# An FFN behind a chunked recurrence on one core: selections on GpSimd that wait for VectorE, C set apart on ScalarE, and a new order of the program

## The chip, the cores and the metric

One core of a Trainium2 chip runs the whole program. The metric is the device time of one execution in microseconds; of several executions the median is taken. TensorE's granted clock was 1.00 throughout the profiled execution.

## What is computed

A state-space recurrence over 4 batches x 8 heads x 768 positions (head size 32, state size 16), in chunks of 32 positions, and then a feed-forward layer over the 3072 tokens of 256 values that it gives. All inputs and the output are fp32. Cut to what matters:

```python
log_a = np.log(np.clip(a, 1e-06, 1.0))
for c in range(nc):                                   # chunks of 32 positions
    cum = np.cumsum(la, axis=-1)
    L = np.exp(cum[:, :, :, None] - cum[:, :, None, :]) * causal
    M = np.einsum('bhin,bhjn->bhij', Cc, Bc) * L
    y_intra = np.einsum('bhij,bhjd->bhid', M, xc)
    y_inter = np.einsum('bhin,bhnd->bhid', Cc, state) * np.exp(cum)[:, :, :, None]
    y[:, :, sl] = y_intra + y_inter
    state = decay_full * state + sum_j (Bc x xc * decay_from_j)
h = x @ w_in                                          # x: y as 3072 x 256; w_in 256 x 2048
g = np.maximum(h, 0.0) + np.log1p(np.exp(-np.abs(h)))
return g @ w_out                                      # w_out 2048 x 256
```

## The kernel before

**Tiling.** The recurrence is cut into 24 units of 128 positions, six for each batch (unit i is batch i // 6, step i % 6). Units 0 to 7 go one by one, from 8 on in pairs. The feed-forward part takes the tokens in six blocks of 512 and the 2048 inner features in 16 tiles of 128. To keep fp32's precision every operand is split into a high and a low part (xh and xl, wih and wil, gh and gl, woh and wol), and each product is three matmuls (high by high, low by high, high by low). Blocks 0 and 1 are done directly; blocks 2 to 5 by a scheme with seven products in place of eight, whose words are a, k, b, c and e.

**What sets the order.** `ORDER` is a string of 1308 words, and the loop at the end of the file calls one function for each word, with the numbers in the word as arguments. Every engine runs its instructions in the order in which the words issue them; across engines only data, buffers and PSUM banks hold things back. `BANKS` gives the PSUM bank of each result. Words that occur several times (D, M, G, P, W and others) run one stage of their function each time.

**The words around the change.** Of a unit i:
- A (`apart`): a copy of C with every other head cleared, parts_c. `A_KIND` says for each unit who does it: "1" VectorE, "0" ScalarE, "2" ScalarE for two units at once.
- S (`score`): the scores of C and B on TensorE, from un (the unit's inputs; head_in for units 0 to 3) and parts_c.
- D (`decays`): the decays with all that is not causal set to zero, rm from fc, by GpSimd's selection: four parts of 128 x 256 for units 0 and 1, two of 128 x 512 for the others. rm has two buffers.
- M (`weigh`): m = scores x rm, two operations on VectorE, one input in PSUM and one in SBUF.
- B and C (`scale_b`, `scale_c`): B and C scaled by decays, bp and cc. T (`spread`): the state at two places, tb. U and N: the state's update. All on VectorE, apart from cc of a few early units.
- R and I (`read`, `within`), for pairs E and J: the output y of a unit on TensorE, from cc and tb, and from m and un.
- G and X, for pairs Y: y times its growth on VectorE (y, yy), the cast to xh on ScalarE, the rest xl = y - xh on VectorE.

Of the feed-forward part: W splits a tile of weights (w and wil or wol on VectorE, wih or woh on ScalarE); H and F are first-layer products, H for 256 of a block's 512 tokens (H2 and H3: feature tiles 2 and 3); P is softplus (e on ScalarE), its cast gh on ScalarE and the rest gl = e - gh on VectorE; Z is a second-layer product; F0.4 is block 0, feature tile 4. Words w, un, v and gg issue loads on SyncE's queue.

All engine operations are recorded at line 173, that of the helper which keeps them in order, so a row is told apart by its tiles.

Of the kernel before, what the change touches and what calls it, by code (L numbers as in the profile page):

```python
# [50 lines left out]
kc B23 ends la warm9 loga loga ft0 lr gb logr logr kb ft0 ft0 ft0 hc0 growth growth fr0 gq0 gq0 hc1 A0 S0 A1 D0  # L51
D0 D0 fr0 fr0 D0 ft0 un0 B0 gq2 hc3 M0 M0 un1 hc2 D1 D1 fr0 C1 warm1 B1 gq2 U0 U0 T1 C2 S1 D1 D1 un6 B6 I0 M1
warm1 G0 M1 U6 fr2 U6 A2 S3 R1 warm1 un4 C4 I1 A4 w2 W2 B4 warm1 warm1 D3 D3 M3 M3 un5 A5 C5 W2 W2 fr2 U1 U1 G1
G1 G0 S2 ft2 ft2 ft2 ft2 ft2 T2 R2 un2 B2 U2 C3 A6 D2 M2 D2 gd M2 I2 un3 B3 U3 U4 X1 U2 G2 T12 U3 S4 U4 warm2 T4
# [65 lines left out]
Z4.14.0 L4.0 ez256.15 es ez256.7 eo256 ez0.7 ez0.15 eo0 C12  # L120
# [886 lines left out]
```

## Time and profile before

| | before |
|---|---|
| median of 3 runs | 313.34 us (313.25 to 313.62) |
| profiled execution | 314.09 us |
| its span | 312.3 us |
| TensorE busy | 305.3 us (98%), 2279 matmuls |
| VectorE busy | 260.6 us (83%), 529 operations |
| ScalarE busy | 180.2 us (58%), 336 operations |
| GpSimd busy | 45.3 us (15%), 62 operations |

1.8 us of the profiled execution lie outside its span. The span has three parts. Up to about 23 us the inputs land, the decays are worked out and the first units of the recurrence run; TensorE's matmuls there are small. From 23 to about 133 us the rest of the recurrence runs between the products of blocks 0 and 1, on all engines. From then to 307 us there are only the feed-forward part's products, with the sums and the splitting that they need. A busy share of an engine is an average over these three, and GpSimd works in the first two alone.

A row of the timeline gives start, duration, engine, operation and tiles; in brackets how long the engine had been idle before it, and what ended that. A longer duration of an operation of the same shape means that it stood still while it ran.

### The profile page before, as it was taken

To read this page: it belongs to the slowest core of one execution; us is meant where nothing else is said; L and a number is where in the kernel's file an instruction comes from. 1 tells how busy PE (TensorE), PEld (TensorE's weight loads), DVE (VectorE), ACT (ScalarE), POOL (GpSimd) and SP (SyncE) were. 2 spreads that over 40 slices of the span, in tenths; PEclk is the share of its full clock that TensorE was granted. 3 is DMA by queue.
4 is the path that set the end of the run, shared out by engine and by line. 5 is a ranking of instruction groups with operands and counts; after the bars stand their busy time and mean duration, and the time that the engine had idled before them with its cause. 6 is when DMAs were issued, how large, how long until landed. Compare 5 with 4: busy or idle time off the path is not lost.

```text
span 312.3 us, 5865 instructions
## 1 busy us (share of the span) xinstructions
PE 305.3 (98%) x2279; PEld 244.4 (78%) x2279; DVE 260.6 (83%) x529; ACT 180.2 (58%) x336; POOL 45.3 (15%) x62
## 2 busy tenths in 40 slices
PE   8989999999999999999999999999999999999995
PEld 4757876887787878788888888888888888888884
DVE  5899999568699799978899968999868888777773
ACT  4947875497235734265754565556655556654561
POOL 1952722302422055000000000000000000000000
PEclk9999999999999999999999999999999999999999
DMA  6989856340653110200010000000001100000003
GB/s 185 315 234 319 277 190 198 111 144 3 188 152 98 56 44 36 70 1 0 0 69 0 0 2 0 1 0 2 0 35 67 36 0 0 1 2 0 0 0 136
DMA packets 14172, 23.21 MB, mean 74 GB/s; under 512 B 1344, under 2 KB 10176, under 8 KB 14144
## 3 DMA queue, kind: packets, MB, share of 16 engines
q1 hardware_dynamic: 14144, 22.84, 22.7%
q8 instruction: 18, 0.29, 0.4%
q14 instruction: 10, 0.08, 0.1%
HBM read 19.29 MB, written 3.54 MB: 73 GB/s over the span
## 4 chain that ended last, share of the span: by engine, by line
PE 62%; DVE 2%; issue 0%
PE sums_at L173 62%; DVE gl L173 0%; DVE xl L173 0%; DVE bp L173 0%; DVE yy L173 0%; DVE parts_c L173 0%; DVE wol L173 0%; DVE end_sum L173 0%
## 5 line engine op out<-in xcount | busy, mean ns | idle before, releaser
L173 DVE TENSOR_TENSOR gl<-e,gh 128x512 fp32r<-128x512 f32 x96 | 65.2, 693 | 19.0 <-ACT gh L173 18.8
L173 PE MATMUL sums_at<-gl,woh 128*128 128x512 f32 (+1 forms) x194 | 75.7, 390 | 0.9 <-DVE gl L173 0.9
L173 PE MATMUL sums_at<-gh,woh 128*128 128x512 f32 (+1 forms) x194 | 76.2, 393 | 0.0
L173 PE MATMUL sums_at<-gh,wol 128*128 128x512 f32 (+1 forms) x194 | 75.2, 388 | 0.0
L173 ACT CAST gh<-e 128x512 fp32r<-128x512 f32 x96 | 58.5, 620 | 22.9 <-PE sums_at L173 17.0
L173 POOL TENSOR_SCALAR_AFFINE_SELECT rm<-fc 128x512 f32<-128x512 f32 (+1 forms) x52 | 44.0, 873 | 77.6 <-DVE m L173 72.1
L173 PEld LDWEIGHTS sums_at<-gl,woh 128*128 128x128 f32 x194 | 36.4, 188 | 10.0 <-DVE gl L173 2.9
L173 PEld LDWEIGHTS sums_at<-gh,woh 128*128 128x128 f32 x194 | 36.4, 188 | 8.2
L173 PEld LDWEIGHTS sums_at<-gh,wol 128*128 128x128 f32 x194 | 36.5, 188 | 7.2
L173 ACT ACTIVATE e<-sums_at 128x512 f32<-128x512 f32 x48 | 28.1, 595 | 24.1 <-PE sums_at L173 23.8
L173 PE MATMUL sums_at<-xh,wih 128*128 128x512 f32 (+1 forms) x104 | 39.7, 381 | 0.8 <-DVE y L173 0.7
L173 PE MATMUL sums_at<-xh,wil 128*128 128x512 f32 (+1 forms) x104 | 39.0, 375 | 0.1
L173 PE MATMUL sums_at<-xl,wih 128*128 128x512 f32 (+1 forms) x104 | 38.8, 373 | 0.0
L173 ACT ACTIVATE e<-e 128x512 f32<-128x512 f32 x48 | 29.9, 630 | 14.1 <-DVE e L173 14.1
L173 DVE TENSOR_TENSOR e<-sums_at,u 128x512 f32<-128x512 f32 x48 | 32.5, 684 | 5.2 <-PE sums_at L173 4.5
L173 DVE TENSOR_TENSOR m<-sums_at,rm 128x512 f32<-128x512 f32 x48 | 31.2, 680 | 2.6 <-PE sums_at L173 2.5
L173 DVE TENSOR_TENSOR u<-sums_at,u 128x512 f32<-128x512 f32 x32 | 21.9, 686 | 3.4 <-PE sums_at L173 2.6
L173 PE MATMUL sums_at<-sxih,sw 128*128 128x512 f32 x64 | 24.6, 389 | 0.0
L173 PEld LDWEIGHTS sums_at<-xh,wih 128*128 128x128 f32 x104 | 19.6, 188 | 5.3 <-DVE y L173 1.5
L173 PEld LDWEIGHTS sums_at<-xh,wil 128*128 128x128 f32 x104 | 19.6, 188 | 4.2 <-DVE wil L173 0.8
L173 PEld LDWEIGHTS sums_at<-xl,wih 128*128 128x128 f32 x104 | 19.6, 188 | 3.3
L173 ACT CAST sw<-sums_w 128x512 fp32r<-128x512 f32 x16 | 9.9, 619 | 17.3 <-DVE sums_w L173 17.3
(115 smaller groups left out, 426.7 us busy)
## 6 DMA issues: line engine op xcount, KB each, us to landing
un<-in_un SPq DMA_DIRECT2D x20, 320.0 KB, 4.1
wraw<-in_w_in SPq DMA_DIRECT2D x8, 511.5 KB, 5.3
wraw<-in_w_out SPq DMA_DIRECT2D x8, 511.5 KB, 4.3
out_t<-o SPq DMA_DIRECT2D x11, 256.0 KB, 2.0
gg<-gd SPq DMA_DIRECT2D x18, 128.0 KB, 4.2
head_in<-in_un SPq DMA_DIRECT2D x4, 192.0 KB, 3.8
head_in<-in_un SPq DMA_DIRECT2D x4, 128.0 KB, 2.5
gd<-lr SPq DMA_DIRECT2D x4, 96.0 KB, 5.1
```

What stands on the lines that cost most here:

```text
L173: return lambda *a, **k: tc.keep_in_program_order(f(*a, **k))
```

## The change

Three things are changed.

**The selections wait.** Each operation that is issued on VectorE is remembered as the last one (`last_of_v`). A selection of the decays of units 2 to 23 gets a dependence, through a semaphore, on the VectorE operation that stands last before it in the program. Before, it waited only for the data and the buffer.

**C is set apart on ScalarE.** `A_KIND` has no "1" left: 11 operations on un and one on head_in go from VectorE to ScalarE.

**The order.** `ORDER` holds the same 1308 words in another order, nearly all of them moved, and `BANKS` other banks.

```diff
-A_KIND = "102200001100101110111011"
+A_KIND = "002200000000000000000000"
...
-    in_order = [False]
+    in_order, last_of_v = [False], [None]
...
             f = getattr(self.engine, name)
+            if self.engine is nc.vector:
+
+                def kept(*a, **k):
+                    last_of_v[0] = f(*a, **k)
+                    return tc.keep_in_program_order(last_of_v[0])
+
+                return kept
             if in_order[0] or self.engine is nc.tensor:
...
-            Pl.affine_select(
+            select = Pl.affine_select(
...
+            if i > 1:
+                tc.add_manual_dep(
+                    select.ins,
+                    last_of_v[0].ins.name,
+                    mybir.DependencyInfo(mybir.DependencyClass.Sync, mybir.DependencyReason.DATA),
+                    reason="beside the next operation of VectorE",
+                )
             yield
...
-R4 T3 R3 I3 w0 W0 w4 W4 D4 D4 M4 M4 W2 I4 X0 gg3 G4 S5 G3 W4 G2 X2 H3 H2 G3 X3 F0.2 F0.3 v9 W4 B9 T5 P0.2 D5 D5
+W4 W4 I3 B6 U6 un5 C5 G2 D5 G2 S4 D5 gg3 T4 X0 H2 A5 U6 G3 G3 M4 M4 R4 I4 X3 v8 B8 X2 S5 G4 F0.2 A8 P0.2 D6 D6
```

In the rows below the number behind a tile's letters is the unit (m4 is m of unit 4) or the block and feature tile (gl0_6), and the last number is a name of the buffer.

VectorE around the xl of unit 0, the last operation that the first product of the feed-forward part needs. Before:

```order
L173 TENSOR_TENSOR tb3_394<-state2_370,kb_75 128x64
L173 TENSOR_TENSOR m4_419<-sums_at_69,rm4_416 128x512 x2
L173 TENSOR_TENSOR wil_77<-w2_269,wih_76 128x2x256
L173 TENSOR_TENSOR xl_0_302<-y0_227,xh_0_301 128x2x128
L173 TENSOR_TENSOR y4_435<-sums_at_69,gg3_432 128x256
L173 TENSOR_TENSOR y3_445<-sums_at_69,gg3_432 128x256
```

After:

```order
L175 TENSOR_TENSOR m2_360<-sums_at_69,rm2_276 128x512 x2
L175 TENSOR_TENSOR wil_77<-w2_232,wih_76 128x2x256
L175 SCALAR_TENSOR_TENSOR w4_344<-wraw4_313,ends1_84 128x512
L175 TENSOR_TENSOR bp6_387<-un6_341,ft0_129 128x128
L175 TENSOR_TENSOR y2_400<-sums_at_69,gg0_131 128x256
L175 TENSOR_TENSOR tb4_417<-state3_256,kb_75 128x64
L175 TENSOR_TENSOR xl_0_284<-y0_330,xh_0_283 128x2x128
L175 COPY state6_427<-sums_at_69 128x64
L175 TENSOR_TENSOR y3_429<-sums_at_69,gg3_414 128x256
L175 TENSOR_TENSOR m4_432<-sums_at_69,rm4_299 128x512 x2
```

The two weighings of unit 4 stood before the xl of unit 0 and now stand behind it, and the first stage of w4 moved ahead of it.

VectorE around the weighings of units 8 and 9. Before:

```order
L173 TENSOR_TENSOR wil_77<-w6_597,wih_76 128x2x256
L173 SCALAR_TENSOR_TENSOR w7_750<-wraw7_748,ends0_83 128x512
L173 TENSOR_TENSOR m9_758<-sums_at_69,rm9_756 128x512
L173 TENSOR_TENSOR m8_760<-sums_at_69,rm8_753 128x512 x2
L173 SCALAR_TENSOR_TENSOR w5_725<-wraw5_723,ends1_84 128x512
L173 TENSOR_TENSOR tb8_773<-state7_698,kb_75 128x64
L173 TENSOR_TENSOR xl_1_562<-y7_668,xh_1_561 128x2x128
L173 TENSOR_TENSOR m9_758<-sums_at_69,rm9_756 128x512
L173 TENSOR_TENSOR wol0_79<-w7_750,woh0_78 128x512
L173 TENSOR_TENSOR gl0_7_817<-e0_7_781,gh0_7_783 128x512
```

After:

```order
L175 TENSOR_TENSOR m8_744<-sums_at_69,rm8_606 128x512
L175 TENSOR_TENSOR xl_1_495<-y7_654,xh_1_494 128x2x128
L175 TENSOR_TENSOR wil_77<-w6_690,wih_76 128x2x256
L175 SCALAR_TENSOR_TENSOR w7_759<-wraw7_757,ends0_83 128x512
L175 TENSOR_TENSOR bp10_764<-un10_737,ft0_129 128x128
L175 TENSOR_TENSOR m9_770<-sums_at_69,rm9_767 128x512 x2
L175 TENSOR_TENSOR m8_744<-sums_at_69,rm8_606 128x512
L175 TENSOR_TENSOR gl0_0_788<-e0_0_602,gh0_0_604 128x512
```

In the new order both selections of unit 9 are issued between this bp10 and the m9 behind it: they wait for bp10, and m9 needs them. In the old order GpSimd had the selections of unit 9 without a wait for an operation of VectorE next to them.

## Rows read from the trace of the kernel before

**Rows 1.** Chain of waits, last long piece: start us, us, engine, tile, line.

```profile
115.72 193.28 PE sums_at L173 x962
```

**Rows 2.** Busy us (and operations) by stretch, then clock, DMA share, GB/s.

```profile
core 0: us, PE busy (x) PEld busy (x) DVE busy (x) ACT busy (x) POOL busy (x), PEclk, DMA share, GB/s
9.00:23.20 14.20, 13.10 (x265) 9.53 (x265) 13.95 (x36) 10.18 (x36) 10.43 (x16) 1.00 0.90 274
23.20:39.20 16.00, 15.77 (x216) 12.88 (x216) 16.00 (x36) 12.54 (x23) 7.78 (x7) 1.00 0.87 296
39.20:50.00 10.80, 10.04 (x91) 7.52 (x90) 10.63 (x21) 6.62 (x12) 3.96 (x4) 1.00 0.61 199
50.00:115.70 65.70, 65.16 (x704) 51.02 (x702) 53.24 (x112) 38.06 (x68) 16.50 (x20) 1.00 0.35 107
115.70:132.70 17.00, 16.98 (x182) 13.33 (x182) 16.78 (x36) 6.13 (x11) 4.20 (x4) 1.00 0.14 48
132.70:307.40 174.70, 174.70 (x773) 143.85 (x769) 144.08 (x274) 102.26 (x179) 0.00 (x0) 1.00 0.03 11
```

**Rows 3.** Timeline of TensorE, first and last of 24 matmuls of 256 columns.

```profile
23.20 0.39 PE L173 MATMUL sums_at<-xh,wih 128*128 128x256 f32 x1 [0.69 <-DVE y L173]
...
26.10 0.28 PE L173 MATMUL sums_at<-xh,wil 128*128 128x256 f32 x1
```

**Rows 4.** Waits of the weight loads, 23.2 to 128 us: total us, times, longest.

```profile
PEld sums_at L173 <- DVE gl L173: 1.9, 3, 1.1
```

**Rows 5.** Timeline of VectorE, 27 to 30 us.

```profile
27.46 1.22 DVE L173 TENSOR_TENSOR wil<-w,wih 128x512 fp32r<-128x512 f32 x1
...
28.80 0.68 DVE L173 TENSOR_TENSOR wil<-w,wih 128x512 fp32r<-128x512 f32 x1
29.41 0.28 DVE L173 TENSOR_TENSOR cc<-un,fr 128x128 f32<-128x128 f32 x1
29.61 0.41 DVE L173 TENSOR_TENSOR y<-sums_at,gg 128x256 f32<-128x256 f32 x1
29.94 0.67 DVE L173 TENSOR_TENSOR gl<-e,gh 128x512 fp32r<-128x512 f32 x1
```

**Rows 6.** Operations on parts_c from un: ns min/median/max, first and last start.

```profile
L173 DVE TENSOR_SCALAR parts_c<-un,kb x11: 270/279/755, 26.8 to 123.6; 128x128 f32<-128x128 f32 x11
L173 ACT ACTIVATE parts_c<-un,kb x9: 377/396/404, 12.9 to 93.1; 128x128 f32<-128x128 f32 x9
```

**Rows 7.** Timeline of VectorE, 46 to 50 us.

```profile
46.12 0.95 DVE L173 TENSOR_TENSOR xl<-y,xh 128x256 fp32r<-128x256 f32 x1
47.00 0.68 DVE L173 TENSOR_TENSOR m<-sums_at,rm 128x512 f32<-128x512 f32 x1
...
48.20 1.19 DVE L173 TENSOR_TENSOR gl<-e,gh 128x512 fp32r<-128x512 f32 x1
```

**Rows 8.** Timeline of GpSimd, from 32 and from 45 us.

```profile
32.69 5.20 POOL L173 TENSOR_SCALAR_AFFINE_SELECT rm<-fc 128x512 f32<-128x512 f32 x3 [4.54 <-DVE m L173]
...
45.08 1.73 POOL L173 TENSOR_SCALAR_AFFINE_SELECT rm<-fc 128x512 f32<-128x512 f32 x2 [6.52 <-DVE m L173]
47.75 2.23 POOL L173 TENSOR_SCALAR_AFFINE_SELECT rm<-fc 128x512 f32<-128x512 f32 x2 [0.93 <-DVE m L173]
```

**Rows 9.** Selections and weighings: ns min/median/max, first and last start us.

```profile
L173 POOL TENSOR_SCALAR_AFFINE_SELECT rm<-fc x52: 442/725/2317, 7.9 to 123.1; 128x512 f32<-128x512 f32 x44, 128x256 f32<-128x256 f32 x8
L173 DVE TENSOR_TENSOR m<-sums_at,rm x48: 673/680/693, 9.1 to 131.2; 128x512 f32<-128x512 f32 x48
```

**Rows 10.** Timeline of VectorE, the xl of unit 0.

```profile
21.89 0.93 DVE L173 TENSOR_TENSOR xl<-y,xh 128x256 fp32r<-128x256 f32 x1
```

**Rows 11.** Timeline of TensorE at 96 us.

```profile
96.14 0.45 PE L173 MATMUL sums_at<-cc,tb 32*64 32x128 f32 x8 [0.37 <-DVE cc L173]
```

**Rows 12.** Softplus and cast on ScalarE: ns min/median/max, first and last start us.

```profile
L173 ACT ACTIVATE e<-sums_at x48: 587/597/606, 26.0 to 289.9; 128x512 f32<-128x512 f32 x48
L173 ACT CAST gh<-e x96: 602/622/630, 27.4 to 303.9; 128x512 fp32r<-128x512 f32 x96
```

More of the change, by code (lines that the diff above doesn't have):

```diff
@@ L50 @@
 ORDER = """
[L51 to L54, printed above, removed]
-R4 T3 R3 I3 w0 W0 w4 W4 D4 D4 M4 M4 W2 I4 X0 gg3 G4 S5 G3 W4 G2 X2 H3 H2 G3 X3 F0.2 F0.3 v9 W4 B9 T5 P0.2 D5 D5
@@ L116 @@
[L116 to L120 removed]
+ends A3 T18 kc la loga loga gb warm9 lr logr logr growth ft0 ft0 gq0 fr0 un2 un1 ft0 B1 ft0 ft0 kb D0 D0 growth
@@ new lines @@
+H1 W1 W1 F0.1 M6 M6 w3 W3 W3 P0.3 P0.3 H0 F0.0 B7 P0.0 P0.0 D8 D8 P0.1 S7 M7 M7 I6 gg6 G6 W1 U7 U7 R7 I7 G7 N8
+N8 T9 S8 S9 w11 w6 W6 W6 W3 W3 fr2 F0.5 Z0.3.0 G6 Z0.3.1 G5 X5 P0.2 P0.2 Z0.2.0 P0.1 P0.1 Z0.1.0 Z0.1.1 T8 w5 W5
+P0.5 W5 v10 C10 Z0.2.1 M8 A10 G7 X7 W6 W6 F0.6 w7 W7 W7 fr2 B10 W7 D9 D9 M9 M9 D10 D10 v13 A13 F0.7 P0.7 M8 P0.0
+E8 J8 N10 P0.6 N10 Z0.0.1 Z0.0.0 X6 W5 F1.6 W7 P0.5 v11 gg8 P0.6 A11 P0.6 Z0.6.0 Z0.6.1 P0.5 W5 P0.7 Z0.5.1 P0.7
+D11 P0.4 P0.4 Y8 w8 W8 Z0.4.0 w14 w9 W8 W8 W8 W14 W9 W9 Z0.7.1 Z0.4.1 K0.1 v14 B14 W14 W14 S10 S11 M11 A14 F1.4
@@ new lines @@
+P1.6 F1.5 P1.4 P1.4 W14 M10 C11 M10 P1.6 Z0.5.0 B13 P1.5 w15 Z0.7.0 K0.0 C14 T10 D11 F1.0 T11 E10 M11 J10 v12
+A12 B12 N12 P1.6 gg10 w10 W10 W9 W9 P1.5 W10 W10 F1.2 P1.2 N12 W10 Y10 F1.1 S12 B11 w12 W12 T14 T13 P1.0 W12 S13
+Z1.6.0 F1.7 P1.2 P1.1 Z1.6.1 v15 A15 B15 C15 P1.5 P1.2 Z1.2.1 D12 D12 Z1.5.1 Z1.2.0 C13 v19 B19 P1.7 M12 M12
+P1.7 P1.7 Z1.7.0 Z1.7.1 D13 D13 M13 M13 P1.1 D15 D15 P1.1 D14 W12 E12 J12 gg12 Y12 S14 S15 P1.0 P1.0 Y8 Y10 Y8
+N14 N14 Z1.1.1 Z1.5.0 W12 Z1.1.0 D14 W11 W11 Y12 F0.13 P0.13 P0.13 M14 W15 F0.10 P0.10 F1.3 F0.14 P1.3 P1.3
@@ new lines @@
+P0.14 Y10 P1.4 Z1.4.1 P1.3 Z1.3.1 M15 Z1.3.0 Z1.0.1 K1.1 v17 M14 T15 E14 M15 J14 v16 A16 B16 N16 D16 D16 A17 S16
+S17 W15 W15 D17 Y14 D17 Z1.0.0 Y14 Y14 P0.13 v18 A18 Z1.4.0 K1.0 C17 v22 N16 T17 C22 F0.15 F0.8 T16 C16 P0.15
+F1.12 P0.15 M16 M16 M17 M17 B22 E16 J16 D18 D18 P1.12 B18 N18 N18 T20 T19 S18 gg18 P0.14 P0.14 D19 gg16 Y16 A19
+S19 M19 F0.11 P0.11 F1.15 P1.15 w13 W13 F0.9 M18 P0.10 M18 W15 Z0.14.1 W13 W13 Z0.14.0 Y12 P0.10 P0.15 v20 C20
+F0.12 P0.12 P0.12 D20 W13 Z0.15.1 Z0.13.1 v21 C21 A21 Z0.13.0 P0.12 Z0.12.1 W11 W11 Z0.10.1 Z0.10.0 xa2.256 P0.9
@@ new lines @@
+P0.9 Z0.12.0 P0.9 P0.11 Z0.9.0 Z0.9.1 C19 E18 P0.11 P0.8 B20 B21 N20 P0.8 D19 M19 J18 Y16 Y16 D20 N22 P1.15 Y18
+P0.8 v23 D22 Z0.11.1 N20 T22 N22 T21 A20 S20 S21 gg20 Y18 M20 Z0.15.0 M20 xa3.256 a1.0.1 k1.0 A23 C23 sw1.0 D21
+D21 Z0.11.0 D22 Z0.8.1 L0.1 M21 M21 F1.11 a1.0.2 Z0.8.0 L0.0 P1.11 F1.8 D23 A22 S22 S23 e1.0.0.0 sw1.0 P1.12
+sw1.0 P1.12 sw1.0 P1.11 P1.11 E20 J20 Y20 P1.8 P1.8 P1.8 a1.1.1 k1.1 F1.14 Z1.12.1 C18 F1.9 P1.9 Y18 P1.15
+Z1.15.1 D23 a1.1.2 e1.1.0.0 Z1.15.0 P1.9 xa4.0 T23 M22 M22 M23 E22 M23 J22 gg22 Y20 xs1.256 Z1.12.0 P1.9 Z1.9.0
@@ new lines @@
+Z1.9.1 xs1.256 P1.14 Z1.8.1 xa3.0 F1.10 P1.10 xa2.0 xs1.0 xs1.0 F1.13 Z1.8.0 P1.13 P1.13 Y22 a1.0.6 P1.10 b1.0
+P1.10 a1.0.5 a1.0.7 a1.2.1 C12 Y22 e1.1.0.0 Z1.10.1 Z1.10.0 e1.1.0.0 Z2.1.1 Z2.1.0 P1.13 Z1.13.0 c1.0 Z1.13.1
+Y20 xa5.0 e1.0.1.1 a1.0.3 a1.0.4 Z1.11.1 k1.2 sw1.1 e1.0.0.0 e1.0.0.0 a1.2.2 P1.14 P1.14 Z1.14.1 Z2.0.0 e1.2.0.0
+a1.3.1 Z1.14.0 sw1.1 sw1.1 L1.1 sw1.2 sw1.1 a1.1.6 e1.0.0.1 Z1.11.0 a1.1.5 e1.2.0.0 e1.2.0.0 Z2.0.1 e1.0.1.0
+L1.0 e1.0.0.1 e1.0.0.1 Z2.2.1 e1.0.1.0 e1.0.1.0 b1.1 k1.3 e1.0.1.1 e1.0.1.1 e1.0.1.0 a1.1.7 Z2.8.0 Z2.2.0 c1.1
@@ new lines @@
+a1.1.4 e1.1.1.1 a1.1.3 Z2.8.1 e1.1.1.1 e1.1.1.1 sw1.2 sw1.2 e1.0.0.1 e1.1.1.0 sw1.2 a1.3.2 e1.0.1.1 a1.2.6
+e1.1.0.1 Z3.0.0 e1.1.1.0 e1.1.1.0 e1.1.1.0 a1.2.7 Z3.8.0 Z2.9.1 Z3.8.1 e1.1.1.1 Z3.9.1 sw1.3 sw1.3 sw1.3 Z3.0.1
+Z2.9.0 sw1.3 a1.2.5 e1.3.0.0 e1.3.0.0 Z3.9.0 e1.1.0.1 b1.2 c1.2 e1.2.1.1 a1.2.4 a1.2.3 a1.4.1 e1.2.1.0 e1.1.0.1
+e1.1.0.1 Z3.1.0 sw1.4 a1.3.6 k1.4 e1.2.1.1 e1.2.1.1 a1.4.2 e1.2.0.1 e1.2.0.1 a1.3.7 Z3.1.1 e1.2.0.1 a1.3.5 xs2.0
+e1.2.1.1 Z3.10.0 Z3.10.1 e1.2.0.1 sw1.4 Z3.2.0 Z3.2.1 T12 e1.4.0.0 a1.5.1 e1.4.0.0 b1.3 c1.3 e1.3.1.1 e1.3.1.1
@@ new lines @@
+a1.3.4 e1.4.0.0 Z2.4.1 a1.3.3 Z2.4.0 sw1.4 sw1.4 a1.4.6 e1.2.1.0 e1.3.1.0 e1.3.1.0 e1.3.0.1 sw1.5 a1.4.7 k1.5
+a1.5.2 e1.3.0.0 Z2.3.1 Z2.3.0 e1.5.0.0 a1.6.1 e1.5.0.0 b1.4 c1.4 a1.4.4 e1.5.0.0 Z2.5.1 a1.4.5 e1.3.1.0 e1.3.1.0
+Z2.11.0 Z2.11.1 e1.3.1.1 e1.3.1.1 Z3.11.0 e1.3.0.1 xs2.0 Z3.11.1 e1.3.0.1 e1.3.0.1 Z3.3.1 k1.6 a1.6.2 sw1.5
+Z2.5.0 sw1.5 e1.2.1.0 e1.2.1.0 e1.4.1.1 e1.4.1.1 a1.4.3 sw1.5 a1.5.6 Z2.10.1 sw1.6 e1.4.1.0 e1.4.1.0 a1.5.7
+e1.4.0.1 b1.5 a1.5.5 e1.6.0.0 a1.7.1 Z2.10.0 c1.5 a1.5.4 e1.5.1.1 e1.4.0.1 a1.5.3 e1.4.1.1 e1.4.1.1 Z3.12.1
@@ new lines @@
+Z3.12.0 e1.4.0.1 e1.4.0.1 Z3.4.1 Z3.4.0 k1.7 a1.7.2 sw1.6 sw1.6 sw1.6 e1.5.0.1 a1.6.5 e1.4.1.0 a1.6.6 e1.5.1.0
+e1.4.1.0 Z2.12.1 Z2.12.0 e1.6.0.0 e1.6.0.0 Z2.6.1 Z2.6.0 e1.5.1.1 e1.5.0.1 e1.5.0.1 e1.5.0.1 e1.7.0.0 a2.0.1
+e1.7.0.0 xa4.256 b1.6 k2.0 sw1.7 sw1.7 sw1.7 sw2.0 Y22 a1.6.7 c1.6 e1.6.1.1 e1.6.1.1 Z3.5.0 a2.0.2 a1.6.4 Z3.5.1
+a1.6.3 sw1.7 e1.5.1.1 a1.7.6 e1.6.1.0 a1.7.7 e1.6.1.0 Z3.3.0 e1.5.1.1 Z3.13.0 Z3.13.1 e1.6.0.1 a1.7.5 e1.7.0.0
+sw2.0 b1.7 c1.7 a1.7.4 Z2.7.1 Z2.7.0 e1.6.0.1 e1.6.0.1 e1.6.0.1 e1.7.1.1 Z3.6.0 e1.5.1.0 e1.5.1.0 e1.6.1.0
@@ new lines @@
+e2.0.0.0 e1.6.1.0 Z3.6.1 e1.5.1.0 Z2.13.0 Z2.13.1 a1.7.3 a2.1.1 xa5.256 e1.7.1.1 e1.7.1.1 e1.7.1.1 Z3.15.1
+e1.7.1.0 e1.7.1.0 sw2.0 Z2.14.1 e1.7.1.0 Z3.15.0 xs2.256 e1.7.1.0 k2.1 a2.1.2 Z2.15.1 e1.6.1.1 sw2.0 e1.7.0.1
+e1.6.1.1 Z3.14.1 e1.7.0.1 xs2.256 e1.7.0.1 e1.7.0.1 a2.0.6 Z3.7.1 a2.0.7 Z2.15.0 sw2.1 sw2.1 a2.0.5 b2.0 c2.0
+e2.0.1.1 L2.1 e2.1.0.0 a2.2.1 k2.2 sw2.1 a2.0.4 e2.0.1.0 e2.0.1.0 Z3.7.0 Z2.14.0 Z3.14.0 sw2.2 L2.0 a2.0.3
+e2.1.0.0 e2.1.0.0 Z4.1.0 sw2.1 a2.1.7 a2.2.2 e2.0.0.1 e2.0.0.0 e2.0.0.1 a2.1.5 e2.0.0.0 sw2.2 e2.2.0.0 a2.1.6
@@ new lines @@
+L3.0 e2.2.0.0 e2.2.0.0 e2.0.1.0 Z4.0.1 Z4.2.0 e2.0.1.1 a2.3.1 Z4.0.0 b2.1 k2.3 e2.0.1.0 Z4.8.1 c2.1 a2.1.4
+Z4.8.0 e2.1.1.1 e2.1.1.1 sw2.2 Z4.1.1 sw2.2 a2.2.6 a2.1.3 e2.0.1.1 e2.0.1.1 Z5.8.1 e2.1.1.0 a2.2.7 sw2.3
+e2.1.0.1 a2.2.5 a2.3.2 e2.1.1.1 e2.1.1.1 Z5.9.1 Z4.2.1 b2.2 c2.2 e2.2.1.1 a2.2.4 a2.2.3 e2.0.0.1 e2.0.0.1 L3.1
+e2.2.1.1 Z5.0.1 sw2.3 sw2.3 sw2.3 e2.2.1.1 e2.2.1.1 e2.3.0.0 Z5.0.0 Z5.8.0 Z5.10.1 sw2.4 a2.4.1 e2.2.0.1 a2.3.5
+Z5.10.0 e2.2.0.1 Z5.9.0 e2.2.1.0 a2.3.7 e2.2.1.0 e2.2.1.0 e2.2.1.0 a2.3.6 e2.3.0.0 e2.3.0.0 k2.4 a2.4.2 Z4.3.1
@@ new lines @@
+Z4.3.0 e2.4.0.0 a2.5.1 b2.3 c2.3 sw2.4 e2.3.1.1 a2.3.4 a2.3.3 e2.1.1.0 e2.1.1.0 e2.1.1.0 Z4.9.0 e2.4.0.0
+e2.4.0.0 Z4.4.0 Z4.4.1 Z4.10.1 k2.5 e2.3.0.1 e2.3.0.1 sw2.4 sw2.4 a2.4.6 a2.4.5 Z4.10.0 e2.3.1.0 a2.4.7 sw2.5
+sw2.5 e2.2.0.1 e2.2.0.1 Z4.9.1 e2.3.0.1 e2.3.0.1 Z5.3.1 Z5.2.0 Z5.3.0 a2.5.2 b2.4 c2.4 e2.3.1.0 e2.3.1.0 sw2.5
+sw2.5 a2.5.6 e2.3.1.0 Z4.11.1 e2.1.0.1 e2.1.0.1 a2.4.4 e2.4.1.1 e2.4.1.1 a2.4.3 e2.1.0.1 e2.4.1.1 B17 Z5.2.1
+Z4.11.0 e2.5.0.0 a2.6.1 e2.5.0.0 e2.4.1.0 a2.5.7 e2.4.1.0 e2.4.1.0 Z5.1.1 e2.4.0.1 sw2.6 sw2.6 sw2.6 e2.4.1.0
@@ new lines @@
+Z4.12.1 Z4.12.0 a2.5.5 e2.4.0.1 e2.4.0.1 b2.5 Z5.1.0 c2.5 e2.3.1.1 e2.5.0.0 Z4.5.0 k2.6 a2.6.2 e2.5.1.1 a2.5.4
+e2.4.0.1 Z5.4.0 e2.4.1.1 Z5.12.0 Z5.12.1 e2.6.0.0 e2.6.0.0 e2.6.0.0 Z4.6.1 a2.7.1 sw2.7 a2.5.3 e2.5.1.0 e2.5.1.0
+e2.5.1.0 Z5.4.1 e2.5.1.0 Z4.13.0 Z4.6.0 sw2.6 a2.6.7 Z4.13.1 e2.5.0.1 e2.5.0.1 a2.6.5 e2.3.1.1 a2.6.6 e2.3.1.1
+Z5.11.0 e2.5.0.1 e2.5.0.1 e2.5.1.1 e2.5.1.1 sw2.7 e2.5.1.1 Z5.13.0 k2.7 a2.7.2 e2.7.0.0 b2.6 c2.6 Z5.5.0 Z5.13.1
+a2.6.4 e2.6.1.1 a2.6.3 sw2.7 sw2.7 a2.7.6 e2.6.1.0 a2.7.7 e2.6.1.1 Z5.11.1 e2.6.1.1 e2.6.1.1 Z5.14.0 e2.6.0.1
@@ L121 @@
+a2.7.5 e2.6.0.1 Z5.5.1 Z5.14.1 b2.7 c2.7 a2.7.4 e2.7.1.1 a2.7.3 e2.6.0.1 e2.6.0.1 Z5.6.0 e2.6.1.0 e2.6.1.0
+e2.6.1.0 Z4.14.0 e2.7.1.0 Z4.14.1 e2.7.1.0 e2.7.1.0 e2.7.1.0 Z4.5.1 Z4.15.0 e2.7.1.1 e2.7.1.1 Z5.6.1 e2.7.1.1
+e2.7.0.0 Z5.15.0 e2.7.0.0 e2.7.0.1 Z4.7.0 L4.0 Z4.15.1 e2.7.0.1 e2.7.0.1 Z4.7.1 L4.1 e2.7.0.1 Z5.7.0 ez256.15
+ez256.7 ez0.7 B23 ez0.15 L5.0 es eo256 eo0
 """
 BANKS = (
-    "0102460230023204633332630124060670247017624072401721172421456712460314214614614412640104510124261121"
-    "2402604526472374506406570"
+    "0102314620231220140206465462046120246010602146012310400461302141240612462232321462320246202014423462"
+    "3304636770343450167016701"
```

68 lines of the change are left out of this document (4 added, 64 removed).

## The prediction

> **What bounds the kernel now.** I read the chain of waits first: it ends in 193.28 us of TensorE alone, from 115.72 us on [rows 1]. The table of stretches agrees: from 132.7 to 307.4 us TensorE is busy without a gap and VectorE for 144 of 174.7 us [rows 2]. Nothing that VectorE or GpSimd gains there moves the end; what counts is how late TensorE already is by then. In that stretch 773 matmuls take 174.70 us, 0.226 us each. I gave every matmul of the program such a pitch (0.226 us for 512 columns, 0.12 for 256, of which 24 begin from 23.20 to 26.10 with two short breaks [rows 3], and for the recurrence's small ones the closest start-to-start that the trace shows) and summed: 295.6 us of work. The start of a matmul less the work ahead of it is its **lag**, what TensorE has lost up to there: an estimate. It is 7.7 us at the first matmul of the feed-forward part (23.20 us), 9.25 where the words of unit 7 are read (36.1), 9.6 at 48.2, 10.7 at 50.0, 11.7 at 96.5, 12.4 at 115.72 and 13.2 at the end. So 5.5 us are lost between 23 and 133 us, and the waits of the weight loads name VectorE's results for most of it, gl above all [rows 4].
>
> Why is VectorE late there? It is busy in 13.95 of 14.20, 16.00 of 16.00 and 10.63 of 10.80 us [rows 2]. But part of "busy" is standing still. A wil takes 0.68 us at 28.80 and 1.22 at 27.46, C's setting-apart up to 0.755 against a median of 0.279, the xl at 46.12 0.95 where a y of that width takes 0.41, the gl at 48.20 1.19 [rows 5 to 7]. They begin while a selection of GpSimd's runs: those of 45.08 and 47.75 lie over the last two [rows 8]. No m, which has one input in PSUM, is ever stretched: 673 to 693 ns in all 48 [rows 9]. I count 20 stretched operations in the whole trace, 8.6 us together, of which 11, with 4.7 us, lie before 50.3 us. The selections stretch as well: the group at 32.69 has three in 5.20 us, where one alone takes 0.72 [rows 8, 9].
>
> **The change, part by part.** The trace of before has VectorE's next operation start some 75 ns ahead of the end of the one before it (the wil of 28.80 takes 0.68 and the next begins at 29.41 [rows 5]), so I take an operation as its duration less that: 0.60 us for m, w, wil, gl, 0.33 for y, 0.20 for bp or cc, 0.13 for tb.
>
> *C apart on ScalarE.* Twelve operations leave VectorE, 11 of 0.279 us and one on head_in; 12 x 0.20 = 2.4 us, spread from 7 to 124 us. Five of the 20 collisions are theirs, about 0.46 us each (the longest 0.755 against 0.279 [rows 6]), 2.3 us more. ScalarE gets 12 x 0.396 us = 4.8 us [rows 6]; it is busy in 38 of 65.7 us from 50 to 115.7 [rows 2], so I cost that at nothing. If a scores' matmul or an e waits for one of them, it is 0.4 us at that place.
>
> *The waits.* A selection now starts when the VectorE operation ahead of it in the source ends, so it runs beside the one behind that. About half of the 22 units' first selections get an m, y or state there, which read PSUM; the others sit out one operation or two. The cost is where the selection stands directly ahead of its own m: VectorE then idles for the selection. This is so for units 9, 11, 12, 13 and 19, and once each. The nearest row is the selection's own 0.725 us (median) [rows 9]; with a hand-over of some 0.1 us (the selection of 47.75 begins 0.07 after the end of the m of 47.00 [rows 7, 8]) I take 0.85 us, 4.2 in all. The bounds: nothing, where VectorE has that much in hand ahead of TensorE's need, and 4.2, where nowhere. GpSimd's queue holds only selections, so a waiting one delays the next selection and through it the next m, not a DMA.
>
> *The new order, up to the first matmul.* From the first m (9.1 us [rows 9]) to the end of the xl of unit 0 (22.8 [rows 10]), VectorE has 34 operations of 11.8 us by the sizes above and needs 13.7. In the new order two weighings (unit 4's) fall behind that xl, and one w moves ahead: 10.4 us. With an m that begins 0.2 later, about 0.5 of collisions (unit 4's selections run into unit 1's xl) and 0.8 of waits for scores, the xl ends at 21.0. TensorE has 14.1 us of work ahead of its first half product instead of 15.5, so the lag there becomes about 7.0 instead of 7.7.
>
> *Up to unit 7's reading.* In the new order 26.1 us of VectorE's work must be done by then and 25.6 of TensorE's; in the old 27.3 and 26.8. VectorE remains the later one in both, so the gain is what VectorE no longer stands still: 2.0 us of collisions from 9 to 30 us go (xl 0.52, C apart 0.47, wil 0.54, tb 0.54), some 0.5 to 0.8 remain or come, the later first m costs 0.2. I take a lag of 8.0 instead of 9.25: **1.2 us**, between 0.3 (half of the collisions come back in other places) and 2.2 (none).
>
> *From 36 to 50 us.* The old kernel loses 1.45 us more here, 1.1 of them when the gl of 48.20 comes 0.5 late out of a collision and its matmul, the longest of the waits, stands still [rows 4, 7]. In the new order the products of this stretch find gl several places earlier, and by the same sums VectorE's work falls 1.1 us behind TensorE's at unit 8's reading (35.3 against 36.4). The wait of 0.85 us for unit 9's selection fits just inside that. I leave 0.35 us lost: **1.1 us** gained, between 0.3 and 1.4.
>
> *From 50 to 132.7 us.* Lost before: 2.5 us, of which cc at 96.14 (behind a stretched tb and cc) and gl at 115.7 make 1.1 [rows 4, 11]. In the new order tb and cc of that unit no longer stand directly behind its selections, but four of the five self-made waits lie here, and at three second-layer products (blocks 1, 0 and 4) only three products, 9 x 0.226 = 2.0 us, stand between a first-layer product and the second-layer one that needs it, while e, gh and gl need 0.60 + 0.62 + 0.68 = 1.9 us [rows 5, 12]. I take **0.5 us** gained, between 0.6 lost and 1.2 gained.
>
> From 132.7 us on both orders feed TensorE without a gap: nothing. Sum: 1.2 + 1.1 + 0.5 = 2.8 us; bounds 0.0 and 4.8. The profiled execution took 314.09 us with a span of 312.3; the median of the runs is 313.34, 0.75 below it. 314.09 - 2.8 = 311.3, and by the median **310.5 us**.
>
> [...] The collisions above show a second operation held up, and the xl at 46.12 took 0.95 us where a full halt to the selection's end (46.82) and 0.41 after it would be 1.11 [rows 7, 8]. [...]
>
> **The rivals.**
> *B, the selections ahead of their own m decide.* Five waits of 0.85 us in VectorE's queue, behind which the gl of the second layer's products stand. For it: VectorE is busy 16.78 of 17.0 us up to 132.7 and 53 of 65.7 before that [rows 2], so it has little to give. It decides if VectorE has less than 0.85 us in hand at each of these. Then 4.2 us are lost against 2.8 gained: 313.34 + 1.4 = **314.7 us**, slower. Against it: from 36 us on I find 0.4 to 1.3 us in hand at each.
> *C, given back between 50 and 133 us.* TensorE is earlier but then waits at the three narrow places and for cc of unit 22, whose load the new order issues shortly ahead of it: 0.6 us, as at 96.14, at three of these, some 1.9 us of the 2.8: **312.4 us**. For it: before had one such place, and the in-order queue delays gl by whatever stands ahead. Against: 1.9 us still fit in 2.0.
> [...]
>
> **Chances.** The forecast 0.56, B 0.20, C 0.14, D 0.10. A measurement of this kernel tells about 0.2%, 0.63 us, from no change, so 312.7 to 314.0 is the same. Faster: nearly all of the forecast's (0.54), most of C and D (0.08 + 0.06): 0.68. Same: the rest of C and D, a quarter of B and a little of the forecast: 0.15. Slower: 0.17. The range goes from the sum's upper bound (313.34 - 4.8 = 308.5, rounded out) to 313.6, which holds C and D and the sum's lower bound, and leaves out most of B.
>
> **What would show it.** The first matmul of the feed-forward part near 21.1 us; VectorE's stretched operations down from 20 to under 8, and no C apart among them; no wait for gl at 48 to 50 us; the end of the chain beginning earlier than 115.72, and FFN matmuls without a gap after 130 us, as now. B would show as five idle stretches of VectorE, released by the selection (rm), each followed by a wait of TensorE for m, gl or yy; C as waits for gl or e at those narrow products; D as as many stretched operations as now. The prediction is wrong first of all if VectorE's idle time before m turns out to be passed on to TensorE, or if the order's feed of loads (un, w) is later than the old one's, which no row here prices.

## The result, and the profile after

| | before | after |
|---|---|---|
| median of the runs | 313.48 us | 310.68 us (310.03 to 311.15, 4 runs) |
| profiled execution | 314.09 us | 310.69 us |
| its span | 312.3 us | 309.0 us |

The ratio is 0.9899, 95% interval 0.9862 to 0.9936: 2.8 us faster, where 310.5 us was predicted. Run again beside the last experiments, the changed kernel took 310.54 us.

The chain of waits of the kernel after ends in a long piece of TensorE alone, as before, but that begins at 46.57 us and no longer at 115.72 [rows 1]. Columns: start us, us, what.

```profile
46.57 259.11 PE sums_at L180 x1676
```

From 46.57 us on the chain names no engine but TensorE. The stretches, cut as in [rows 2] but for the first ends, say the same: TensorE busy without a gap from 50 us, and VectorE idle for 2.4 us already between 36 and 50.

```profile
9.00:21.20 12.20, 10.96 (x221) 7.83 (x217) 12.16 (x32) 8.85 (x32) 7.27 (x12) 1.00 0.87 290
21.20:36.00 14.80, 14.63 (x248) 12.02 (x247) 14.29 (x35) 12.65 (x26) 5.67 (x8) 1.00 0.96 312
36.00:50.00 14.00, 13.58 (x108) 10.76 (x108) 11.60 (x25) 11.76 (x22) 3.24 (x4) 1.00 0.67 203
50.00:115.70 65.70, 65.70 (x710) 52.16 (x709) 51.69 (x109) 37.59 (x70) 17.35 (x21) 1.00 0.32 103
115.70:132.70 17.00, 17.00 (x184) 13.46 (x183) 16.25 (x31) 8.59 (x17) 3.93 (x5) 1.00 0.14 50
```

The waits of the weight loads up to 128 us (total us, times, longest) have gl at 0.4 in place of 1.9 [rows 4]:

```profile
PEld sums_at L180 <- ACT e L180: 1.1, 3, 0.7
PEld sums_at L180 <- DVE bp L175: 1.0, 2, 0.7
...
PEld sums_at L180 <- DVE gl L175: 0.4, 2, 0.2
```

The tiles answer to [rows 6] and [rows 9] (ns min/median/max). No selection takes 2.3 us any more, no gl 1.19, all of C is set apart on ScalarE, and m is as untouched as it was:

```profile
L180 POOL TENSOR_SCALAR_AFFINE_SELECT rm<-fc x52: 442/725/1217, 7.1 to 127.2; 128x512 f32<-128x512 f32 x44, 128x256 f32<-128x256 f32 x8
L175 DVE TENSOR_TENSOR m<-sums_at,rm x48: 674/684/693, 9.0 to 130.1; 128x512 f32<-128x512 f32 x48
L175 DVE TENSOR_TENSOR gl<-e,gh x96: 678/685/805, 31.9 to 302.8; 128x512 fp32r<-128x512 f32 x96
L180 ACT ACTIVATE parts_c<-un,kb x20: 386/398/417, 10.1 to 119.7; 128x128 f32<-128x128 f32 x20
```

Counted as in the prediction, 11 operations of VectorE are stretched, 4.2 us together, where before 20 were, with 8.6 us. TensorE's lag, an estimate as before, summed with the same pitches:

| lag of TensorE, us | before | after | gained so far |
|---|---|---|---|
| first matmul of the feed-forward part (23.20; after 20.99) | 7.67 | 6.85 | 0.8 |
| unit 7 read (36.06; after 33.53) | 9.25 | 7.97 | 1.3 |
| about 50 us | 10.70 | 8.69 | 2.0 |
| last unit's products (131.7; after 131.46) | 12.77 | 9.13 | 3.6 |
| end | 13.24 | 9.91 | 3.3 |

The profiled executions differ by 3.4 us, the medians by 2.8; the table explains the former.

### The profile page after: what moved, and what is told of

It reads as the page before. It is cut to its first block, busy times and chain, and to the rows that moved or that the text cites. A ratio compares the mean times of both kernels' runs of the same rounds, so it can differ in the third digit from the quotient of the medians.

```text
span 309.0 us, 5900 instructions
## 1 busy us (share of the span) xinstructions
PE 302.7 (98%) x2279; PEld 243.1 (79%) x2279; DVE 256.0 (83%) x517; ACT 183.6 (59%) x348; POOL 40.6 (13%) x62
## 4 chain that ended last, share of the span: by engine, by line
PE 93%; DVE 2%; POOL 2%; ACT 1%; issue 1%; POOLq 0%; DVEq 0%; ACTq 0%
PE sums_at L180 93%; POOL rm L180 2%; DVE m L175 1%; ACT L180 0%; DVE kc L175 0%; POOL kc L180 0%; ACT e L180 0%; DVE w L175 0%; DVE wil L175 0%; ACT fc L180 0%; DVE end_sum L175 0%; DVE y L175 0%; ACT la L180 0%; POOL keep L180 0%; DVE bp L175 0%
## 5 line engine op out<-in xcount | busy, mean ns | idle before, releaser
L175 DVE TENSOR_TENSOR gl<-e,gh 128x512 fp32r<-128x512 f32 x96 | 64.4, 688 | 15.2 <-ACT gh L180 14.7
L180 POOL TENSOR_SCALAR_AFFINE_SELECT rm<-fc 128x512 f32<-128x512 f32 (+1 forms) x52 | 39.3, 778 | 85.3 <-DVE bp L175 28.6
```

Source lines behind the costliest of these rows:

```text
L175: last_of_v[0] = f(*a, **k)
L180: return lambda *a, **k: tc.keep_in_program_order(f(*a, **k))
```

## Experiments

**The three parts alone and in pairs.** First the changed kernel with one part undone, and the old one with C apart alone. Without the dependences:

```diff
-            if i > 1:
+            if i > NU * NB:
                 tc.add_manual_dep(
```

> The changed kernel without the selections' dependences: new order, new banks, C apart on ScalarE, but a selection starts as soon as its data and buffer are there. Theory (VectorE's collisions are what TensorE loses, and the dependences keep most of them away): the stretched operations go from 10 back to 15 or more, 6 us or more of VectorE's time, and the time rises by 1 to 2.5 us over the changed kernel's 310.7, to about 312.3. Rival 1 (the new order alone brings the gain): 310.7 within 0.4. Rival 2 (the dependences cost more than they bring, since VectorE idles 0.85 us before m at five places): 310.0 or less.

Measured: 316.87 us (316.82 to 317.19), ratio to before 1.0108 (1.0084 to 1.0132). The direction is the theory's, the size is not: 6.2 us slower than with the dependences, and rivals 1 and 2 fall. VectorE's timeline between 19 and 27 us shows why:

```profile
19.90 1.19 DVE L175 SCALAR_TENSOR_TENSOR w<-wraw,ends 128x512 uint32<-128x512 uint32 x1
21.01 0.79 DVE L175 TENSOR_TENSOR bp<-un,ft 128x128 f32<-128x128 f32 x1
...
24.57 0.80 DVE L175 TENSOR_TENSOR bp<-un,ft 128x128 f32<-128x128 f32 x1
25.29 0.92 DVE L175 TENSOR_TENSOR xl<-y,xh 128x256 fp32r<-128x256 f32 x1
```

and GpSimd's the selections that they ran into, each let go by an m that freed its buffer:

```profile
19.45 2.23 POOL L180 TENSOR_SCALAR_AFFINE_SELECT rm<-fc 128x512 f32<-128x512 f32 x2 [1.01 <-DVE m L175]
24.46 1.50 POOL L180 TENSOR_SCALAR_AFFINE_SELECT rm<-fc 128x512 f32<-128x512 f32 x2 [2.78 <-DVE m L175]
```

A lone bp takes 0.28 us; these take 0.79 and 0.80. In the whole trace 28 operations are stretched, 12.6 us together. Twelve of them, 5.8 us, lie between 13 and 40 us, 4.8 us more than in the changed kernel, and TensorE's lag at the read of unit 7 is 11.97 us in place of 7.97: most of what VectorE loses there arrives at TensorE.

With the dependences, but C set apart as before:

```diff
-A_KIND = "002200000000000000000000"
+A_KIND = "102200001100101110111011"
```

> The changed kernel with C apart as before: new order, dependences, but 12 operations of 0.28 us back on VectorE. Theory: VectorE is the later engine only up to about 36 us, where 4 of the 12 lie; 4 x 0.20 = 0.8 us at most and collisions of some of them, so 311.0 to 311.6. Rival (VectorE has enough in hand and C apart is worth nothing): 310.7 within 0.3.

Measured: 317.73 us (316.18 to 318.82). Both theory and rival are wrong. In the trace (an execution of 316.30 us) the lag up to 90 us is that of the changed kernel (8.5 against 8.8). The loss comes at 97 to 119 us: the new order issues A of unit 19 directly ahead of its scores, and on VectorE that stands behind a gl and a yy. TensorE's and VectorE's timelines:

```profile
99.07 0.50 PE L180 MATMUL sums_at<-parts_c,un 32*128 32x128 f32 x8 [1.78 <-DVE parts_c L175]
```

```profile
97.40 0.68 DVE L175 TENSOR_TENSOR gl<-e,gh 128x512 fp32r<-128x512 f32 x1
98.00 0.69 DVE L175 TENSOR_TENSOR yy<-sums_at,gg 128x512 f32<-128x512 f32 x1
98.60 0.42 DVE L175 TENSOR_SCALAR parts_c<-un,kb 128x128 f32<-128x128 f32 x1
```

The scores of unit 21 wait in the same way, 1.50 us up to 119.16. Between the two, after the first of these waits, TensorE's granted clock is at half (columns as in [rows 2]):

```profile
100.60:103.90 3.30, 3.30 (x9) 2.58 (x8) 1.57 (x3) 0.60 (x1) 0.00 (x0) 0.50 0.00 0
```

Matmuls of 512 columns begin 0.43 us apart there in place of 0.226; eight of them cost some 1.6 us more. So of the 5.6 us between this execution and the changed kernel's profiled one, 3.3 are the two waits and 1.6 the clock. Four of the other executions had a lower mean granted clock (0.987 to 0.989, against 0.995 here) and took 317.6 to 318.8 us: part of the 7.1 us between the medians is the clock's too. So what ScalarE does for C in this kernel is not to spare VectorE 2.4 us but to have C apart in time. With both undone:

> New order and banks alone: C apart as before (12 operations back on VectorE), no dependences. Theory (collisions): 312.8, some 0.5 us above the new order with C on ScalarE, as the five stretched operations on C come back too; at most 0.7 us below the kernel before. Rival 1 (order alone): 310.7 to 311.0. Rival 2: 310.3.

Measured: 323.06 us (319.61 to 323.62), far above the theory and both rivals. Here the clock takes more: in the trace, of the execution of 323.62 us, it is at half from 13.7 to 20.4 us and once more from 126.4 to 129.6.

```profile
13.70:20.40 6.70, 6.70 (x84) 4.17 (x84) 5.55 (x12) 2.20 (x7) 2.98 (x4) 0.50 0.73 228
```

Only the execution of 319.61 us had a mean granted clock of 1.000; it is 8.9 us above the changed kernel and some 6 above the one before. So the new order alone is no gain but a loss of 6 to 10 us, and whether the losses of the two parts (6.2 and 7.1) add up can't be read from these medians. And C on ScalarE in the old kernel:

> The kernel before with C apart on ScalarE and nothing else changed: old order, old banks, no dependences. Theory: the two stretched operations on C at 26.8 and 37.9 us (0.74 and 0.71 us) leave VectorE while it is the late engine, and most of that reaches TensorE unless the selection then collides with the next operation: 312.3 to 313.0. Rival (the selection stretches the next operation instead, or VectorE is not the cause): 313.4 within 0.3.

Measured: 315.37 us (314.42 to 316.19), ratio 1.0057 (1.0038 to 1.0076): slower, which neither had. Two things in its trace, that of the longest of the ten executions (316.19 us). The operation for unit 0 stands in ScalarE's queue where TensorE needs it at once, and costs 1.0 us at the start (the product of by_head begins at 9.91 us, in the old kernel at 8.91):

```profile
9.47 0.50 PE L173 MATMUL sums_at<-parts_c,head_in 32*128 32x128 f32 x8 [0.60 <-ACT parts_c L173]
```

And the collisions did not go with the operations that had them: 21 operations are stretched, 9.0 us, where it was 20 with 8.6. The selections of 27 to 36 us meet other ones:

```profile
29.03 1.19 DVE L173 TENSOR_TENSOR wil<-w,wih 128x512 fp32r<-128x512 f32 x1
30.15 0.79 DVE L173 TENSOR_TENSOR cc<-un,fr 128x128 f32<-128x128 f32 x1
...
33.99 0.94 DVE L173 TENSOR_TENSOR xl<-y,xh 128x256 fp32r<-128x256 f32 x1
34.86 1.19 DVE L173 SCALAR_TENSOR_TENSOR w<-wraw,ends 128x512 uint32<-128x512 uint32 x1
```

Then the dependences in the old order, with the new `A_KIND` and without:

> The old order and banks with C apart on ScalarE and with the dependences. In the old order nearly every selection is issued directly ahead of the m that needs it, which cost nothing as long as it could start when its buffer was free. Theory (the dependence keeps collisions away only in an order that issues the selections early enough; here VectorE waits for rm 0.85 to 1.6 us at some 20 places, half of them before 50 us, where TensorE follows): 318 to 330. Rival (the dependences alone are what helps): 311 to 312.

> The kernel before with the dependences alone: old order, old banks, C apart as before. Theory, as for the old order with C on ScalarE: 318 to 330, within 2 us of it. Rival (the dependences alone are what helps): 311 to 312.5.

Measured: 331.75 us (331.47 to 332.41) and 334.20 (332.14 to 334.75); the theory, a little beyond its range. Part of that is the clock, whose mean was 0.979 to 0.995 in the first and 0.969 to 0.990 in the second; the 2.5 us between the two medians are therefore not to be read as the worth of C. VectorE's waits from 9 to 150 us, of the one with the new `A_KIND` and then of the dependences alone:

```profile
DVE m L175 <- POOL rm L180: 22.8, 25, 2.2
```

```profile
DVE m L175 <- POOL rm L180: 23.6, 26, 2.2
```

The eight combinations, medians in us:

| | neither | C on ScalarE | dependences | both |
|---|---|---|---|---|
| old order | 313.3 to 313.9 | 315.4 | 334.2 | 331.8 |
| new order | 323.1 | 316.9 | 317.7 | 310.6 |

No part alone gains, and no pair: only the three together. The losses of 323.1, 317.7, 331.8 and 334.2 us hold some of the clock, as said. The banks went with the order in every run and were not tried apart.

**What the collisions cost in all.** The selections of units 2 to 23 were left out of both kernels, in `decays`; every unit is then weighed with decays kept from unit 1 (cut to what matters):

```diff
+        if i > 1:
+            mid[i]["rm"] = kept_rm[0]
+            return
...
```

> The kernel before without the selections of units 2 to 23, in the same way (units weighed with one half of unit 1's masked decays). Theory (the old kernel's loss is the collisions): 8.6 us of stretched operations go, 4.7 of them before 50 us, where TensorE follows VectorE nearly one to one, and 1 us of the later ones: 308.5 to 310.0. Rival (the old order itself feeds TensorE late; collisions are hidden): 312.0 or more.

> The changed kernel without the selections of units 2 to 23 (44 operations on GpSimd left out, with their dependences): every unit is weighed with one half of unit 1's masked decays, so the decays of the other units are left out of the result. VectorE's operations keep their number, shapes and operands. Theory: what the selections still cost in the new order (3.6 us of stretched operations, 4.5 us of VectorE waiting for rm) lies mostly where VectorE has time in hand: 309.6, at most 1.5 us below the changed kernel. Rival B of the prediction (the waits for rm are on TensorE's path): 307.5 or less.

Measured: the old kernel 310.05 us (309.10 to 310.75), the changed one 310.17 (309.31 to 313.29). The first falls by 3.8 us against the 313.86 of before on the same chip, just above the theory's range and far from the rival. In the old kernel's trace VectorE never waits for a selection, so these 3.8 us are the collisions'. No xl or gl of it is stretched any more (gl at most 0.694 us), and gl no longer stands among the long waits of the weight loads:

```profile
L173 DVE TENSOR_TENSOR xl<-y,xh x8: 411/418/419, 16.8 to 45.7; 128x256 fp32r<-128x256 f32 x8
```

```profile
PEld sums_at L173 <- DVE gl L173: 0.2, 1, 0.2
```

The second falls by only 0.5 us against the changed kernel, less than its runs scatter, and the two were not run side by side: as ratios to the old kernel run beside each they are 0.9906 (0.9875 to 0.9936) and 0.9899. Without selections the two orders take the same time within this measurement. So the gain is collisions kept away; of its own the new order shows none, and what the selections still cost in it can't be told from nothing.

**Are the waits ahead of m paid for?** In the changed kernel VectorE waits for rm from 9 to 150 us (total us, times, longest):

```profile
DVE m L175 <- POOL rm L180: 4.5, 7, 0.9
```

The dependences of the five units that stand directly ahead of their own m were left off:

```diff
-            if i > 1:
+            if i > 1 and i not in (9, 11, 12, 13, 19):
```

> The changed kernel with the dependences left off for units 9, 11, 12, 13 and 19, whose selections stand directly ahead of their own m. Theory (VectorE has that time in hand there): 310.7 within 0.5; VectorE's waits for rm fall from 6 to about 2, and three to five operations are stretched in their place. Rival B (the waits for rm are on the path): 309.5 or less. Rival 2 (a selection let go early collides with what stands ahead): 311.5 or more.

Measured: 312.28 us (311.81 to 313.91), 1.6 slower: rival 2. The same stretch of VectorE's timeline in the changed kernel and in this one:

```profile
59.26 0.28 DVE L175 TENSOR_TENSOR cc<-un,fr 128x128 f32<-128x128 f32 x1
59.47 0.35 DVE L175 TENSOR_TENSOR tb<-state,kb 128x64 f32<-128x64 f32 x2
60.52 0.69 DVE L175 TENSOR_TENSOR m<-sums_at,rm 128x512 f32<-128x512 f32 x1 [0.70 <-POOL rm L180]
61.12 0.28 DVE L175 TENSOR_TENSOR bp<-un,ft 128x128 f32<-128x128 f32 x1
61.32 0.69 DVE L175 TENSOR_TENSOR gl<-e,gh 128x512 fp32r<-128x512 f32 x1
61.92 0.69 DVE L175 TENSOR_TENSOR wol<-w,woh 128x512 fp32r<-128x512 f32 x1
```

```profile
59.30 1.41 DVE L175 TENSOR_TENSOR tb<-state,kb 128x64 f32<-128x64 f32 x2
60.63 0.68 DVE L175 TENSOR_TENSOR m<-sums_at,rm 128x512 f32<-128x512 f32 x1
61.23 0.28 DVE L175 TENSOR_TENSOR bp<-un,ft 128x128 f32<-128x128 f32 x1
61.43 1.20 DVE L175 TENSOR_TENSOR gl<-e,gh 128x512 fp32r<-128x512 f32 x1
62.55 1.19 DVE L175 TENSOR_TENSOR wol<-w,woh 128x512 fp32r<-128x512 f32 x1
```

One wait of 0.70 us was there in place of four collisions of 2.1 us (1.06 on the two tb, 0.51 on gl and on wol). TensorE's lag rises by 1.4 us between 46 and 64 us, in the changed kernel by 0.3.

**Smaller edits.** C apart of unit 0 back on VectorE (`A_KIND` "1022" and zeros):

> The changed kernel with one operation back on VectorE: C apart of unit 0 (one operation on head_in, at about 7.5 us). With C apart as before, TensorE was 0.34 us less late than in the changed kernel from the first units to 90 us, since ScalarE's queue came to the row factors 0.3 us sooner. Theory (the start is ScalarE's, that one operation accounts for it): 310.35, 0.2 to 0.5 us below the changed kernel. Rival (the 0.34 us come from another of the twelve, or are made up for later): 310.7 within 0.2.

Measured: 311.01 us (310.41 to 312.67): no gain to be seen. The 0.34 us were scatter: the lag at the first read of a unit is between 5.1 and 5.7 us in traces whose programs are alike up to there. The changed kernel and, beside it, the one with unit 4's selections later:

> The changed kernel once more, unchanged, beside the other three: 310.7, and how far its executions scatter. Its profile also tells whether TensorE's lag at the first units (6.2 at 19 us in its first profile, 5.1 to 5.8 in experiments that differ only later) is scatter of the loads' landing: theory, yes, some 0.5 us either way.

```diff
-G1 W2 S3 M3 warm1 M3 D4 D4 U4 U4 C2 w4 X1 I0 warm2 gd G0 G0 S2 un6 A6 W4 ft2 R2 ft2 ft2 ft2 M2 R3 M2 I2 W2 ft2
+G1 W2 S3 M3 warm1 M3 U4 U4 C2 w4 X1 D4 I0 warm2 gd G0 D4 G0 S2 un6 A6 W4 ft2 R2 ft2 ft2 ft2 M2 R3 M2 I2 W2 ft2
```

> The changed kernel with the two selections of unit 4 moved in the order: behind the xl of unit 1 and behind the first y of unit 0, so that they run beside a y and the two m of unit 2 and no longer beside that xl. Theory (a collision before 36 us reaches TensorE one to one): the xl's 0.54 us go, lag at unit 7's reading 0.3 to 0.5 lower, time 310.3. Rival (the start is set by loads and other waits): 310.7 within 0.2.

Measured: 310.54 us (310.12 to 310.80, 4 runs) and 309.99 (309.51 to 311.81, 6 runs). The xl is at 0.41 us again, as the first row of VectorE's timeline shows, against 0.95 at 16.07 in the changed kernel:

```profile
15.74 0.41 DVE L175 TENSOR_TENSOR xl<-y,xh 128x256 fp32r<-128x256 f32 x1
...
21.96 0.42 DVE L175 TENSOR_TENSOR y<-sums_at,gg 128x256 f32<-128x256 f32 x1 [1.94 <-DMA gg<-gd]
```

The profiled execution is the longest of the six, 311.81: there a load of gg landed late, and VectorE waited 1.94 us for it, which the changed kernel's profiles do not have. The other five are 309.5 to 310.4. The 0.55 us between the medians is what the theory wanted, but the ranges overlap: it is likely, not shown. Its median is the lowest of the kernels that leave no work out.

## Why the prediction was right

The time and the sign hold, and in the main the mechanism: fewer collisions of VectorE with the selections, at waits that TensorE does not see. By its own steps:

*C apart on ScalarE*, costed as 2.4 us less work and 2.3 us fewer collisions on VectorE at no cost elsewhere: wrong as a reason, without harm to the sum. Alone it made the old kernel 2 us slower, since the selections met other operations in place of those on C (21 stretched, 9.0 us, where it was 20 with 8.6); in the new order the kernel is 5.6 to 7.1 us longer without it, 1.6 of that or more by the clock, because A stands there directly ahead of the scores.

*The waits.* That VectorE has the 0.85 us in hand from 36 us on was right: by the lag none of the waits for rm moves TensorE by more than 0.2 us, and taking those of the five units away costs 1.6 us. There are seven waits of 4.5 us in all, where five with 4.2 us were predicted.

*Up to the first matmul* 21.0 us was predicted, 20.99 measured; the lag 7.0, measured 6.85. That it came out so closely is luck. One collision was named there, unit 1's xl, and it came (0.95 us at 16.07, 0.54 lost); but a cc at 11.11, beside the selection of 11.10, was stretched as well, 0.85 us in place of 0.28, so that the collisions took 1.1 us in place of 0.5. Of the 0.8 us of waits for scores none came behind the first m. And it was not the xl of unit 0 that let TensorE begin: it had ended at 20.76 us, and by the chain of waits a bp let TensorE go at 20.01 us, and from there to 32.75 its own matmuls follow one another (start us, us, what):

```profile
19.75 0.21 DVE bp L175
...
20.01 12.74 PE sums_at L180 x174
```

*Up to unit 7's reading* a lag of 8.0 was predicted, 7.97 measured: 1.3 us for 1.2.

*From 36 to 50 us* 1.1 us was predicted and 0.7 came. The collision on gl is gone. What the term lacked was ScalarE: the new order has the second half of the exponentials (fr2) at 40 us, where before it was at 62, and a table load of 1.28 us before and behind it. The second one delays e, and with it an update that TensorE waits for:

```profile
44.62 1.28 ACT L180 ACT_TABLE_LOAD   x1 [1.50 <-PE sums_at L180]
45.92 1.09 ACT L180 ACTIVATE e<-sums_at 128x512 f32<-128x512 f32 x2
```

```profile
46.57 0.32 PE L180 MATMUL sums_at<-un,bp 128*32 128x64 f32 x8 [0.42 <-ACT e L180]
```

The lag rises from 8.06 to 8.66 us there. In the old order the same two loads cost TensorE nearly nothing (lag 11.0 at 62 us and 11.1 at 69).

*From 50 to 132.7 us* 0.5 us was predicted and 1.6 came: the term most out. I had charged the three narrow places with 2.0 us against 1.9 and four of the waits, and expected TensorE to lose two of the old 2.5 us again (2.1 of which lie before 131.7). It lost 0.4. At those narrow places the lag does not move (8.94 at the first, 8.95 at the second, 9.66 before and after the third, that of block 4, which comes later than this stretch), so 1.9 us did fit in 2.0, and rival C falls.

*After 132.7 us* nothing was forecast, and 0.3 us of gain were given back, in six waits for gl of 1.3 us in all against five of 1.0 before.

The errors of the terms leave 3.3 us in the profile in place of 2.8. That the median fell by 2.8, as forecast, is luck in part: the prediction took it to lie 0.75 us below the profiled execution, as before, and after the change the two are alike (310.68 and 310.69). In the chances, the parts named add up to 0.17 for the same and 0.15 for slower, the other way round than written.

Rival B falls with the five let go. Rival D's sign, as many stretched operations as now, did not come: 11 in place of 20 (under 8 were foreseen: that sign failed). But four of the 11 stand beside a selection that had been stretched itself: a tb at 24.19 us, an xl at 75.59, a cc at 105.29 and a tb at 127.67, each 0.51 us longer, half of the 4.2 us. The four selections took 1.03, 1.22, 1.05 and 1.12 us, where one alone takes 0.72. On VectorE the cc at the start, the collision foreseen and the first of these four:

```profile
11.11 0.85 DVE L175 TENSOR_TENSOR cc<-head_in,fr 128x128 f32<-128x128 f32 x1
...
16.07 0.95 DVE L175 TENSOR_TENSOR xl<-y,xh 128x256 fp32r<-128x256 f32 x1
...
23.60 0.68 DVE L175 TENSOR_TENSOR wil<-w,wih 128x512 fp32r<-128x512 f32 x1
24.19 0.73 DVE L175 TENSOR_TENSOR tb<-state,kb 128x64 f32<-128x64 f32 x1
```

And on GpSimd the selections beside the last two of them:

```profile
16.04 0.72 POOL L180 TENSOR_SCALAR_AFFINE_SELECT rm<-fc 128x512 f32<-128x512 f32 x1
...
23.84 1.03 POOL L180 TENSOR_SCALAR_AFFINE_SELECT rm<-fc 128x512 f32<-128x512 f32 x1 [1.81 <-DVE y L175]
```

The selection let go at 23.84, when wil had begun, sat wil out, took 1.03 us in place of 0.72, and held up the tb behind.

The operations with an input in PSUM that were expected beside the selections are stretched neither before nor after: m takes at most 0.693 us in both, y 0.423 and 0.421, a state 0.283 and 0.282. m takes at most 0.692 without the dependences and with the five let go. C's setting-apart, with one tile and one column of factors from SBUF, was stretched to 0.755 [rows 6]. An operation that is held up does not stand still for all that is left of the selection: the xl of 16.07 begins with 0.69 us of its selection left and loses 0.54, the tb of 24.19 with 0.67 left loses 0.51.
